# Key chunk 3 of the first stage loaded through ScalarE's queue, and tile 0's keys by four chunks first

## The chip, the cores and the metric

The kernel runs on one core of a Trainium2 chip. The core has TensorE (PE: matmuls, with a separate row PEld for weight loads), VectorE (DVE), ScalarE (ACT), GpSimd (POOL) and SyncE (SP), which here does nothing but issue DMAs. ScalarE issues a few DMAs as well. All DMAs run on the core's 16 DMA engines. The metric is the device time of one execution in microseconds (us); lower is better. Before the change it is 273.6 us, the median of 3 runs (273.55 to 273.61).

## What is computed

x is 2048 x 640, all tensors are bf16. The output mixes two blocks with a gate per row:

```python
g = sigmoid((x * gate_w).sum(-1, keepdims=True))
a = A(x, wqkv, wo)      # linear attention, 32 heads of 20
b = (gelu(x @ w_gate) * (x @ w_up)) @ w_down
out = g * a + (1 - g) * b
```

In A, `x @ wqkv` gives q, k and v. With phi(t) = (t + 1 where t > 0, else exp(t)) + 1e-6, the attention is phi(q) @ (phi(k)^T v), divided by phi(q) @ sum(phi(k)), and then multiplied by wo. Only the keys phi(x @ wk) and the queries phi(x @ wq) of the first few row tiles, and the gate column, matter for this change.

## The kernel before, in words

x is cut into 16 row tiles of 128 rows, and its 640 columns into 5 chunks of 128 (KC). The contraction over the 640 columns is a sum of 5 matmul steps, one for each chunk; chunk k needs the k-th 128 rows of the weight (`load_wk(k)`, 160 KB) and the transposed tile of x. Tile 0 of x is loaded as it is (`load_x(0)`) and transposed by PE (`T`, line 432) and copied back by VectorE; tiles 1 to 15 are transposed by the DMA itself (`load_xT(i)`, line 354).

The work is written out once in program order and sorted into one list for each engine; every operation waits on semaphores for exactly the operations whose results it needs, and each DMA has its own semaphore. So the order of the calls in the source is the order in which each engine works, and each engine takes its list strictly in order: a PE step that waits for a load holds up all PE steps behind it. The loads without `"act"` are issued by SP, those with `"act"` by ScalarE's queue.

The stages: the start (warm-up matmuls, tile 0's transposes, lines 510 to 514), then the keys of tiles 0 to 3 and the queries of tiles 0 to 3 (KM and QM, lines 451 to 479), then keys and queries together for tiles 4 to 15 (KQ, line 538), then the products of keys with x, the small matrices, the gated feed-forward block (line 706) and the output (line 880). Keys and queries of a tile use two banks of PSUM each (`slot`), eight banks for four results in flight; after the last chunk ScalarE takes the exponential (`phi1`, line 481) and VectorE the maximum (`phi2`, line 491).

`KM(n, ks)` is the step to follow: for tile n (n below 4) and each chunk k in `ks` it issues two matmuls, 512 and 128 columns wide (lines 459 and 460), with the transposed tile as the weights. It waits for the tile's transposed load and for the key chunks in `ks`. `gate_col` (line 502) is one small matmul that needs the gate vector and sets a column of the query weights that all query matmuls wait for. Before the change the loads that matter stand in this order:

- SP: x tile 0, key chunk 0, transposed tile 1, key chunk 3, key chunk 4, transposed tiles 2 and 3, the five query chunks, transposed tiles 4 to 15, and then the large weights.
- ScalarE: a small load of 16 rows (line 368), key chunks 1 and 2, one exponential that brings in its table (line 379), the gate vector (line 381).

And PE's order: chunks 0, 1, 2 of tile 0; chunks 0, 1, 2 of tile 1; chunk 3 of tile 0, chunk 3 of tile 1; the gate column; chunk 4 of tile 0, chunk 4 of tile 1; then tiles 2 and 3 whole.

Of the kernel before, what the change touches and what calls it, by code (L numbers as in the profile page):

```python
# [162 lines left out]
def bass_gated_mix__linear_attn_block__geglu_ffn__prompt_kernel(  # L163
# [63 lines left out]
    with (  # L227
# [8 lines left out]
        with contextlib.ExitStack() as stack:  # L236
# [105 lines left out]
            def dma_in(dst, src, writes, reads=(), eng="sp"):  # L342
                P.op(eng, lambda e, dst=dst, src=src: e.dma_start(dst, src),  # L343
                     reads=reads, writes=writes, dma=new_dma_key())
# [6 lines left out]
            def load_wk(k, eng="sp", after=()):  # L351
                dma_in(wk[:, k, :], A_wqkv[k * 128:(k + 1) * 128, 640:1280], [r_wk[k]], reads=after, eng=eng)

            def load_xT(i, after=()):
                P.op("sp", lambda e: e.dma_start_transpose(xT[:, :, i * 128:(i + 1) * 128],  # L355
                                                           A_x[0, i * 128:(i + 1) * 128, :]),
                     reads=list(after), writes=[r_xT[i]], dma=new_dma_key())
# [12 lines left out]
            load_x(0)  # L370
            load_wk(0)
            load_xT(1)
            load_wk(3)
            load_wk(4)
            load_wk(1, "act")
            load_wk(2, "act")

            zero = nc.const_aps.tensor(0.0, (128, 1), F32)
            P.op("act", lambda e: e.activation(eg[:, 0:1], zero, ACT.Exp), writes=[r_eg[0]])
# [41 lines left out]
            def warm(count, n):  # L421
                def fn(e):
                    last = None
                    for w in range(count):
                        last = e.matmul(ps[:, 4, 0:n], one_l, one_r[:, 0:n], start=True, stop=True)
                    return last
                P.op("pe", fn, writes=[bank[4]])
# [4 lines left out]
            def slot(n):  # L432
                return SLOTS[n % 4]
# [17 lines left out]
            def KM(n, ks):  # L451
                i = seq[n][1]
                b0, b1 = slot(n)

                def fn(e):
                    last = None
                    for k in ks:
                        lhs = xT[:, k, i * 128:(i + 1) * 128]
                        e.matmul(ps[:, b0, :], lhs, wk[:, k, 0:512], start=(k == 0), stop=(k == KC - 1))  # L459
                        last = e.matmul(ps[:, b1, 0:128], lhs, wk[:, k, 512:640],  # L460
                                        start=(k == 0), stop=(k == KC - 1))
                    return last
                P.op("pe", fn, reads=[r_xTa[i] if i < NXN and ks == [0] else r_xT[i]] + [r_wk[k] for k in ks],
                     writes=[bank[b0], bank[b1]])
# [37 lines left out]
            def gate_col():  # L502

                P.op("pe", lambda e: e.matmul(ps[:, 7, 0:5], gw_sb, ident[:, 0:5], start=True, stop=True),
                     reads=[r_gw, r_ident], writes=[bank[7]])
                P.op("dve", lambda e: e.tensor_copy(wq[:, :, 640:641], ps[:, 7, 0:5].unsqueeze(2)),
                     reads=[bank[7]], writes=[r_gcol])
# [4 lines left out]
            T(0, [0], 7)  # L512
            T(0, [1, 2, 3, 4], 6)
            warm(2, 128)
            for k in range(3):
                KM(0, [k])
            for k in range(3):
                KM(1, [k])
            KM(0, [3])
            KM(1, [3])  # L520
            gate_col()
            KM(0, [4])
            KM(1, [4])
            ALLK = list(range(KC))
            for n in range(2 * NQ):
# [419 lines left out]
```

## Time and profile before

| | us |
|---|---|
| median of 3 runs | 273.6 (273.55 to 273.61) |
| the profiled execution | 273.49 |
| its span | 272.2 |
| PE busy | 267.0 |
| DVE busy | 140.9 |
| ACT busy | 76.0 |
| first key matmul (tile 0, chunk 0) | 4.45 |
| first matmul of tile 1's keys | 5.90 |
| first matmul of tile 2's keys | 8.10 |
| first query matmul | 10.82 |

The profiled execution is one run under the hardware profiler; its span runs from the first to the last instruction, and the time outside it is 1.29 us. Times inside the span are counted from its start. In a row of the timeline the columns are start, length, engine, line of the kernel, operation, output and input, count, and in brackets how long the engine was idle before and what ended that. `SPq` and `ACTq` are the queues of SP and ScalarE, whose rows are the issue of a DMA and not the transfer; a row "DMA" in the chain is the time from an issue's start to the landing that released the next step. Line 343 is the helper that all plain loads go through, line 355 that of the transposed ones.

### The profile page before, as it was taken

The numbers are of one execution on the slowest core, as the hardware profiler recorded it, in microseconds if no ns is written. First come the engines' busy times: TensorE is split into PE (matmuls) and PEld (weight loads), VectorE is DVE, ScalarE is ACT, GpSimd is POOL, SyncE is SP. The second block draws the span as 40 slices with busy tenths as digits, with TensorE's granted clock in tenths as the row PEclk, the third lists the DMA queues.
The fourth block names the chain that finished last, engine by engine and source line by source line (L and its number), as shares of the span: only waits on it lengthen the run. The fifth ranks groups of instructions, "written<-read, shape, count | busy, mean of one in ns | idle before, by whom it ended". The sixth has DMA issues, their size and how long they took to land.

```text
span 272.2 us, 3462 instructions
## 1 busy us (share of the span) xinstructions
PE 267.0 (98%) x1366; PEld 127.2 (47%) x1392; DVE 140.9 (52%) x248; ACT 76.0 (28%) x132; POOL 30.6 (11%) x30
## 2 busy tenths in 40 slices
PE   7999999999999999999999999999999999999997
PEld 3555555544445454444444444444444444444444
DVE  1678989997234335999999999634110000000200
ACT  2455555210422453332222232224011122121021
POOL 6000000003240002242332421000000000000000
DMA  7976999610200011614121221262031110110221
GB/s 192 203 117 120 356 401 379 117 3 19 58 19 2 23 52 48 198 28 52 24 48 29 46 48 25 60 233 94 2 78 40 39 39 19 41 39 19 58 60 39
DMA packets 42680, 23.61 MB, mean 87 GB/s; under 512 B 32167, under 2 KB 41255, under 8 KB 42535
## 3 DMA queue, kind: packets, MB, share of 16 engines
q1 hardware_dynamic: 42333, 23.05, 32.2%
q10 hardware_dynamic: 330, 0.33, 0.4%
q8 instruction: 11, 0.18, 0.3%
q14 instruction: 6, 0.05, 0.1%
HBM read 13.67 MB, written 2.63 MB: 60 GB/s over the span
## 4 chain that ended last, share of the span: by engine, by line
PE 96%; DMA 1%; SPq 1%; issue 1%; DVE 0%
PE ps L706 41%; PE ps L880 23%; PE ps L545 12%; PE ps L602 6%; PE ps L859 4%; PE ps L684 2%; PE ps L474 2%; PE ps L827 2%; PE ps L605 1%; DMA pool<-in_A_x_dram 1%; PE ps L459 1%; PE ps L840 1%; SPq L343 1%; SPq L355 0%; PE ps L755 0%
## 5 line engine op out<-in xcount | busy, mean ns | idle before, releaser
L706 PE MATMUL ps<-pool 128*128 128x512 bf16 x509 | 112.8, 379 | 0.7 <-issue 0.2
L706 PEld LDWEIGHTS ps<-pool 128*128 128x128 bf16 x520 | 50.6, 98 | 60.3
L880 PE MATMUL ps<-pool 128*128 128x512 bf16 (+2 forms) x300 | 62.2, 366 | 0.5 <-issue 0.2
L712 ACT ACTIVATE pool<-ps 128x512 f32<-128x512 f32 x52 | 31.1, 597 | 72.8 <-PE ps L706 70.1
L714 DVE TENSOR_TENSOR pool<-ps,pool 128x512 bf16<-128x512 f32 x52 | 34.7, 688 | 31.1 <-PE ps L706 29.8
L880 PEld LDWEIGHTS ps<-pool 128*128 128x128 bf16 x306 | 29.2, 98 | 33.4 <-issue 0.4
L863 DVE TENSOR_TENSOR pool<-ps,pool 128x512 bf16<-128x512 f32 x4 | 2.8, 692 | 61.5 <-PE ps L859 59.4
L545 PE MATMUL ps<-pool 128*128 128x512 bf16 (+1 forms) x176 | 32.5, 343 | 0.2
L770 POOL TENSOR_TENSOR pool<-pool 128x640 f32<-128x640 bf16 x16 | 22.5, 1406 | 72.6 <-DVE pool L772 65.8
L887 ACT ACTIVATE pool<-ps,pool 128x512 bf16<-128x512 f32 (+1 forms) x16 | 10.9, 681 | 68.6 <-PE ps L880 68.6
L545 PEld LDWEIGHTS ps<-pool 128*128 128x128 bf16 x180 | 17.6, 98 | 15.0
L564 DVE SCALAR_TENSOR_TENSOR pool<-ps,pool 128x128 bf16<-128x128 f32 (+2 forms) x36 | 21.7, 603 | 2.1
L555 ACT ACTIVATE pool<-ps 128x640 bf16<-128x640 f32 x24 | 16.9, 704 | 15.8 <-DVE pool L564 9.3
L602 PE MATMUL ps<-pool 128*128 128x512 bf16 x76 | 19.2, 379 | 0.1
L780 DVE TENSOR_TENSOR pool<-pool 128x640 bf16<-128x640 bf16 x16 | 13.2, 825 | 0.6
L778 DVE TENSOR_SCALAR pool<-pool 128x32 f32<-128x32 f32 x16 | 12.8, 802 | 0.6
L772 DVE TENSOR_REDUCE pool<-pool 128x32 f32<-128x640 f32 x16 | 12.9, 807 | 0.0
L650 DVE TENSOR_TENSOR pool<-pool 128x640 f32<-128x640 f32 x14 | 11.6, 825 | 0.5
L859 PE MATMUL ps<-pool 128*128 128x512 bf16 x51 | 11.4, 379 | 0.0
L652 POOL PARTITION_ALL_REDUCE pool<-pool x1 | 4.0, 3972 | 60.2 <-DVE pool L650 60.2
L602 PEld LDWEIGHTS ps<-pool 128*128 128x128 bf16 x78 | 6.9, 98 | 7.3
L561 DVE TENSOR_SCALAR pool<-pool 128x640 bf16<-128x640 bf16 x24 | 7.8, 326 | 1.7 <-ACT pool L555 0.4
(73 smaller groups left out, 123.4 us busy)
## 6 DMA issues: line engine op xcount, KB each, us to landing
out_dram<-pool SPq DMA_DIRECT2D x19, 128.0 KB, 1.7
pool<-in_B_w_gate_dram SPq DMA_DIRECT2D x1, 2080.0 KB, 14.3
pool<-in_B_w_up_dram SPq DMA_DIRECT2D x1, 2080.0 KB, 18.4
pool<-in_A_wqkv_dram SPq DMA_DIRECT2D x8, 160.0 KB, 3.0
pool<-in_A_x_dram SPq DMA_DIRECT2D x1, 1280.0 KB, 9.3
pool<-in_A_x_dram SPq DMA_DIRECT2D x1, 1120.0 KB, 6.4
pool<-in_B_w_down_dram SPq DMA_DIRECT2D x1, 1120.0 KB, 6.2
pool<-omg_row SPq DMA_DIRECT2D x1, 1024.0 KB, 4.8
```

The source lines that it names most:

```text
L545: last = e.matmul(ps[:, b + p, 0:c1 - c0], xT[:, k, i * 128:(i + 1) * 128], wkq[:, k, c0:c1], start=(k == 0), stop=(k == KC - 1))
L555: P.op("act", lambda e: e.activation(e_buf[m], ps_flat[:, o:o + 640], ACT.Exp), reads=banks, writes=[r_e[m]])
L564: P.op("dve", lambda e, c0=c0, c1=c1: e.scalar_tensor_tensor(dst[:, c0:c1], ps_flat[:, o + c0:o + c1], 1.0 + EPS, e_buf[m][:, c0:c1], ALU. ...
L602: last = e.matmul(ps[:, b, :], pk[i][:, c * 128:(c + 1) * 128], x_aug[:, i, 0:512], start=(i == 0), stop=(i == NT - 1))
L706: last = e.matmul(ps[:, b, :], w[:, k, fc * 128:(fc + 1) * 128], xT[:, k, j * 512:(j + 1) * 512], start=(k == 0), stop=(k == KC - 1))
L712: P.op("act", lambda e: e.activation(ge[n], ps[:, gb, :], ACT.Gelu_apprx_tanh), reads=[bank[gb]], writes=[r_ge[n]])
L714: P.op("dve", lambda e: e.tensor_tensor(hT[fc][:, j * 512:(j + 1) * 512], ps[:, ub, :], ge[n], ALU.mult), reads=[bank[ub], r_ge[n]], write ...
L770: P.op("pool", lambda e: e.tensor_tensor(tmp[n], pq[i], z_b, ALU.mult), reads=[r_pq[i], r_zb], writes=[r_tmp[n]])
L772: P.op("dve", lambda e: e.tensor_reduce(den[n], tmp[n].rearrange("p (h d) -> p h d", h=32), AX.X, ALU.add), reads=[r_tmp[n]], writes=[r_de ...
L780: P.op("dve", lambda e: e.tensor_tensor(pq[i].rearrange("p (h d) -> p h d", h=32), pq[i].rearrange("p (h d) -> p h d", h=32), den[n].unsqu ...
L859: last = e.matmul(ps[:, b, :], wd[:, fc, 512:640], hT[fc][:, j * 512:(j + 1) * 512], start=False, stop=(fc == NFC - 2), skip_group_check=True)
L880: last = e.matmul(ps[:, pb, 0:c1 - c0], lhs, rhs, start=False, stop=(q == len(rows) - 1), skip_group_check=True)
```

## The change

Two edits. Key chunk 3 is issued by ScalarE's queue, behind chunks 1 and 2 and ahead of the table's exponential and the gate vector; SP issues chunk 4 directly behind the transposed tile 1. PE's order of the first two tiles becomes chunks 0 to 3 of tile 0, chunks 0 to 3 of tile 1, chunk 4 of tile 0, the gate column, chunk 4 of tile 1. The matmuls and the loads are the same ones, and so many.

```diff
@@ -370,10 +370,10 @@
             load_x(0)
             load_wk(0)
             load_xT(1)
-            load_wk(3)
-            load_wk(4)
             load_wk(1, "act")
             load_wk(2, "act")
+            load_wk(3, "act")
+            load_wk(4)
 
@@ -512,14 +512,13 @@
             T(0, [0], 7)
             T(0, [1, 2, 3, 4], 6)
             warm(2, 128)
-            for k in range(3):
+            for k in range(4):
                 KM(0, [k])
             for k in range(3):
                 KM(1, [k])
-            KM(0, [3])
             KM(1, [3])
+            KM(0, [4])
             gate_col()
-            KM(0, [4])
             KM(1, [4])
```

## The prediction

> **What bounds the kernel now.** I read the page first, for what the whole is limited by; then the chain that ended last, in its first 20 us, where the edited lines lie; then the timeline of SP, ACT and PE there; last the DMA view, cut into short windows. The page says:
>
> ```profile
> span 272.2 us, 3462 instructions
> ...
> PE 96%; DMA 1%; SPq 1%; issue 1%; DVE 0%
> ```
>
> TensorE (PE) makes 96% of the chain of work that ended last (and its busy row has 267.0 us, 98% of the span). The change neither adds nor removes a matmul, so only PE's waits can move the time. The chain shows the one that counts:
>
> ```profile
> 3.06 0.57 SPq L343
> 3.64 0.04 issue
> 3.68 0.43 SPq L343
> 4.11 0.04 issue
> 4.15 3.90 DMA pool<-in_A_x_dram
> 8.05 0.05 issue
> 8.10 0.39 PE ps L459
> ```
>
> Columns are start, length, what. SP, done with the transposed load of x tile 1 (issued from 1.71 to 3.01), issues key chunk 3 (3.06), key chunk 4 (3.68) and x tile 2 (4.15). Tile 2 lands 3.90 us after its issue began, at 8.05, and from 8.10 on the chain is PE alone, apart from 0.05 us steps. Whatever the change is worth stands in the place of that 8.10: the first matmul of tile 2's keys. PE's timeline has the waits before it:
>
> ```profile
> 5.26 0.22 PE L460 MATMUL ps<-pool 128*128 128x128 bf16 x1
> 5.90 0.39 PE L459 MATMUL ps<-pool 128*128 128x512 bf16 x1 [0.42 <-DMA pool<-in_A_x_dram]
> ...
> 6.18 0.38 PE L459 MATMUL ps<-pool 128*128 128x512 bf16 x1
> ...
> 7.78 0.22 PE L460 MATMUL ps<-pool 128*128 128x128 bf16 x1
> ...
> 8.09 0.10 PEld L459 LDWEIGHTS ps<-pool 128*128 128x128 bf16 x1 [0.43 <-DMA pool<-in_A_x_dram]
> ```
>
> Tile 0's first three chunks end at about 5.31; tile 1 lands at 5.85 and its first matmul starts at 5.90; one chunk of one tile takes 6.18 - 5.90 = 0.27 us; the last of the first seven chunks and the gate column ends at about 7.84, and PE then idles until tile 2 is there. The third thing to see is what the DMA engines do meanwhile. q1 is SP's queue, q10 ScalarE's; the columns are packets, MB and time as a share of 16 engines, first in the window from 4.00 to 4.25, then from 4.5 to 5.0:
>
> ```profile
> q10 hardware_dynamic: 55, 0.06, 65.5%
> q1 hardware_dynamic: 79, 0.02, 35.5%
> ```
>
> ```profile
> q1 hardware_dynamic: 393, 0.12, 127.3%
> ```
>
> and all queues together, in the last two columns here (DMA share, GB/s):
>
> ```profile
> 3.00:5.00 2.00, 1.52 (x13) 0.98 (x11) 0.65 (x2) 0.68 (x2) 1.67 (x7) 1.00 1.10 303
> 5.00:5.50 0.50, 0.48 (x4) 0.14 (x2) 0.00 (x0) 0.00 (x0) 0.43 (x1) 1.00 0.96 226
> 5.50:6.85 1.35, 0.95 (x7) 0.57 (x8) 0.00 (x0) 0.00 (x0) 0.00 (x0) 1.00 1.02 257
> ```
>
> From 3.0 to 6.85 the engines' share is 0.96 to 1.10: what waits there waits for engines, not for an issue.
>
> **The change part by part.** First, SP's queue. Chunk 3's issue, 0.57 + 0.04 us, goes, but chunk 4 now comes straight behind the transpose and takes over the 0.57 that the first plain load there cost, in place of 0.43. So tile 2's issue starts at 3.68 and not 4.15: 0.47 us earlier, and with it tile 3 (5.39 to 4.92), the five query chunks and the twelve transposes behind them. These later ones are hidden in either case: tile 3's keys start at 9.47, more than a step after tile 2's, and the query matmuls at 10.82, and no PE wait on a load is listed after 8.10. Without that cover the 0.47 would be a gain there, not a cost.
>
> Second, ScalarE's queue. The two plain loads issued there took 0.93 us together from 1.23, so chunk 3 is issued at about 2.17 and holds ScalarE's queue 0.47 us. Behind it are the table load (2.20, becomes 2.67, ends 3.95), the gate vector's DMA (2.27, becomes 2.74) and one exponential of a zero (3.49, becomes 3.96). The next ScalarE work is at 7.76 after 4.07 us of idle, which hides all of it; with no such idle it would cost the 0.47. The gate vector's few packets were read by 5.0 (no packet of q10 after that); 0.47 later and behind 128 more packets they are read by about 6, and the gate column, which PE reaches at about 7.6, has more than 1 us to spare. Were that gone, PE would wait, and with it chunk 4 of tile 1.
>
> Third, the landing of chunk 3. ScalarE's two chunk loads landed 3.3 us after their issue, so chunk 3 lands at about 2.17 + 3.3 = 5.47 instead of behind tile 1. The new order puts tile 0's fourth chunk ahead of tile 1: it starts at about 5.5, ends at 5.78, and lies in the idle stretch from 5.31 to 5.90. That takes 0.27 us out of what PE still has to do after tile 1's landing: 7.84 - 5.90 - 0.27 = 1.67 us. Chunk 4 (SP's loads of this kind took 3.1 us: 3.06 + 3.1 = 6.2) is wanted about 1.1 us after tile 1's first matmul, so it isn't the last to come.
>
> Behind it on the way to PE's query work stand ScalarE's exponential and VectorE's maximum of tile 1 (VectorE ends at 10.77, PE needs the bank at 11.10): 0.33 to spare, of which a later end of tile 1's keys (7.92 in place of 7.84, below) takes 0.08.
>
> So tile 2's first matmul starts at the later of two moments: tile 2's landing + 0.05, or tile 1's landing + 0.05 + 1.67. Before, the first was 8.10. The second breaks even when tile 1 lands at 6.38.
>
> Fourth, tile 1's landing. Its 640 packets of 256 bytes were read on q1 up to about 5.0, the last half us with q10 nearly empty. Now chunk 3's 128 packets stand on q10 beside them. In the mixed slice above q10 moved 55 packets and q1 79 in 0.25 us; alone, q1 moved 393 in 0.5, or 197 in 0.25. 128 packets at 55 per 0.25 us take 0.58 us, in which q1 loses (197 - 79) x 0.58 / 0.25 = 274 packets, 0.35 us at its own rate. Tile 1 then lands at 6.20. The ends: no delay (5.85), if chunk 3 is fitted in; and all 640 packets at the mixed rate, 640 / 79 x 0.25 = 2.03 in place of 1.24 us, 0.79 late (6.64). I take 0.35, since it is the two measured rates. PE's second moment is then 6.20 + 1.72 = 7.92.
>
> Fifth, tile 2's landing. Low end: it keeps its 3.90 us from issue, 3.68 + 3.90 = 7.58 (the shortest landing of any transpose of x, 3.0, would make it 6.68, and tile 1 then decides). High end: the transposes lose 0.79 to the shared queues and get back nothing, 8.05 + 0.79 = 8.84. Between: what the engines must move before tile 2 is the same bytes in both kernels (tile 0, five key chunks, tile 1, only one of them on another queue), and the engines were occupied all through, so it lands where it did; the unused 4% of 5.0 to 5.5 is 0.02 us. I take 7.95, near to that end, since occupied engines are what the rows show, with a tenth of a us off for the slow 226 GB/s of that stretch, which a second queue might fill. Start of tile 2's keys: the later of 8.00 and 7.92, so 8.00, a gain of 0.1 us.
>
> Here a rule stands against the purpose of such a move. The rows are the engines' shares of 0.96 to 1.10 above. The Trainium skill, page "DMA: Bandwidth & Descriptors", section "Issuing engines are not separate DMA queues", says that loads issued from different engines end up on the same 16 DMA engines and that a second issuer saves only issue time. By the page alone the gain is at most the saved issue, 0.47 us, and nothing where the engines are the limit.
>
> The sum: the profiled execution took 273.49 (span 272.2 and 1.29 around it), 0.11 below the median of 273.6. 273.49 - 0.1 = 273.39, or 273.5 in terms of the median.
>
> **The rivals.** First: tile 2 follows its issue after all. For it speaks that transposes landed between 3.0 and 4.4 us after issue (median 3.6), whatever the queue held, so the 3.9 of tile 2 is not the least. Then the start is the later of 7.63 and tile 1's 7.57 to 7.92: gains of 0.2 to 0.47 us, 273.1 to 273.4. To be faster by over 0.2% (0.55 us, about what a measurement of this kernel can tell from no change) tile 1 would have to land before 5.83 too; with both at the median 3.6 (5.3 and 7.28) the start would be 7.33 and the time 272.85. Against: tile 1 gets more company, not less.
>
> Second, on the other side: the transpose pays for the shared engines twice. Chunk 3's packets hold up tile 1 by the upper 0.79, and since tile 2 stands behind tile 1 on q1, it is late by as much while the place chunk 3 left on q1 brings nothing. Tile 2 lands at 8.84, its keys start 0.79 later: 274.4. It loses from a landing of tile 2 past 8.05 on, and shows past 8.60. For it: 0.5 us after tile 1's packets (5.0 to 5.5) only 226 GB/s moved with engines at 0.96, so a transpose leaves something behind that slows others. Against: the place on q1 is a whole chunk of 128 packets.
>
> Third: it doesn't do what it says, chunk 3 landing so late on ScalarE's queue that tile 0's fourth chunk, now ahead of tile 1, holds PE. It costs only past 8.10 - 0.05 - 1.67 - 0.27 = 6.11, 0.64 later than expected; before, chunk 3 came from SP 3.2 us after a later issue. At 6.5 it would be 0.4 slower: 274.0.
>
> PE's clock is no rival with a price: it idled 0.48 us before the first key matmul (4.45) and 0.42 before 5.90 and each chunk after it still took 0.27; the new idle, 5.78 to 6.25, is as long.
>
> **How the numbers follow.** Forecast, start between 7.8 and 8.3 (273.3 to 273.8): 0.5. First rival: 0.2, half past the bound. Second: 0.22, nearly all past the bound. Third: 0.08, half past it at its end. So faster 0.1, same 0.65, slower 0.25. The range reaches to the first rival's lower part and the second's price: 272.95 to 274.4, which leaves some 0.15 outside. The forecast's own range is 273.3 to 273.8.
>
> **What would show it.** Right: chunk 3's issue in ScalarE's queue at 2.2; SP's transpose of tile 2 at 3.7; tile 0's fourth chunk on PE at about 5.5, before the wait for tile 1; tile 1's first matmul near 6.25; tile 2's near 8.0; all later PE work shifted by the same. Wrong: tile 2's first matmul below 7.6 (issue was the limit) or above 8.6 (second rival), a wait of PE on a key chunk after 6.1 (third), or any difference that arises after 20 us, where I expect only a shift.

## The result, and the profile after

The changed kernel takes 274.51 us (median of 14 runs, 273.88 to 278.61) against 273.5 before (14 runs, 273.14 to 273.66). The ratio is 1.0049, with a 95% interval of 1.003 to 1.0067: it is 0.49% slower. The ratio leaves out the run of 278.61, which counts as slow, and it is not the ratio of the two medians, which are 0.37% apart. Two things are to be explained: the median, and the spread, since the 14 runs before lie within about 0.5 us and those after within several. Four of the five runs at 275.5 and above were recorded with a mean granted clock of 0.994 or 0.988, all others with 1.00.

The profiled execution took 274.37 us. Its page has

```profile
span 273.1 us, 3462 instructions
...
PE 96%; DMA 2%; issue 1%; ACTq 0%; DVE 0%
```

so the span is 0.9 us longer and the DMA has 2% of the chain that ended last instead of 1%. That chain, in its first us (start, length, what):

```profile
1.71 0.46 ACTq L343
2.20 4.64 DMA pool<-in_A_wqkv_dram
6.88 0.39 PE ps L459
```

It no longer leads through SP and tile 2 but through ScalarE's queue: key chunk 3 is issued there at 2.20, as planned, and lands 4.64 us later, at 6.84. PE's timeline shows who waits:

```profile
5.29 0.39 PE L459 MATMUL ps<-pool 128*128 128x512 bf16 x1 [0.19 <-DMA pool<-in_A_wqkv_dram]
5.52 0.22 PE L460 MATMUL ps<-pool 128*128 128x128 bf16 x1
6.88 0.39 PE L459 MATMUL ps<-pool 128*128 128x512 bf16 x1 [1.15 <-DMA pool<-in_A_wqkv_dram]
...
8.52 0.17 PE L504 MATMUL ps<-pool 128*128 128x5 bf16 x1
...
8.82 0.38 PE L459 MATMUL ps<-pool 128*128 128x512 bf16 x1
```

The row at 6.88 is tile 0's chunk 3, which PE now has ahead of all of tile 1. The matmul at 8.82 is the first of tile 2's keys, the one that stood at 8.10: 0.72 us later. The first query matmul moved from 10.82 to 11.54, also 0.72, and the shift stays at 0.71 up to 49 us. There, at the start of the products of keys with x, the span gains another 0.15 us (the wait of PE's weight load for VectorE is 0.47 and not 0.15). That step also turns up in the run with tile 1 loaded plainly, below, which loses nothing in the first stage, so I don't count it as a part of the loss.

The landings in this execution, for what was issued around 2.2 us (KB each, us from issue to landing):

```profile
pool<-in_A_wqkv_dram ACTq DMA_DIRECT2D x1, 160.0 KB, 4.6
pool<-in_A_x_dram SPq DMA_TRANSPOSE x1, 5.3
```

Before, ScalarE's chunk loads took 3.3 us and tile 1's transpose 4.1. Both are late now, by 1.3 and 1.2 us. What the two queues did from 4.25 to 5.75 us (packets, MB, time as a share of 16 engines):

```profile
q1 hardware_dynamic: 588, 0.17, 65.2%
q10 hardware_dynamic: 129, 0.15, 62.3%
```

and the window of all queues (last two columns: DMA share, GB/s), first after, then before:

```profile
4.25:5.75 1.50, 1.15 (x6) 0.39 (x6) 0.01 (x1) 0.00 (x0) 1.04 (x3) 1.00 1.28 213
```

```profile
4.25:5.75 1.50, 1.03 (x6) 0.43 (x6) 0.00 (x0) 0.00 (x0) 1.05 (x3) 1.00 1.15 262
```

62.3% of 16 engines over 1.5 us is 14.95 us for 129 packets: 116 ns for one, on average over the queue, whose packets are mostly the 1280-byte rows of the chunks. In the slice that the prediction took its rate from, before the change, it was 65.5% of 16 x 0.25 us for 55 packets, 48 ns. So the queue's packets took 2.4 times as long, and the engines moved less in all, 213 GB/s against 262, while they counted as busier (1.28 against 1.15).

### The profile page after: what moved, and what is told of

Same layout as the page of the kernel before. It is cut to its first block, busy times and chain, and to the rows that moved or that the text cites. A ratio compares the mean times of both kernels' runs of the same rounds, so it can differ in the third digit from the quotient of the medians.

```text
span 273.1 us, 3462 instructions
## 1 busy us (share of the span) xinstructions
PE 267.1 (98%) x1366; PEld 127.1 (47%) x1392; DVE 140.8 (52%) x248; ACT 75.9 (28%) x132; POOL 30.6 (11%) x30
## 4 chain that ended last, share of the span: by engine, by line
PE 96%; DMA 2%; issue 1%; ACTq 0%; DVE 0%
PE ps L705 41%; PE ps L879 23%; PE ps L544 12%; PE ps L601 6%; PE ps L858 4%; DMA pool<-in_A_wqkv_dram 2%; PE ps L683 2%; PE ps L474 2%; PE ps L826 2%; PE ps L604 1%; PE ps L459 1%; PE ps L839 1%; PE ps L754 0%; PE ps L475 0%; PE ps L460 0%
```

## The experiments

Two theories of the lateness stood against each other at first: the loads (the chunk on ScalarE's queue and the transpose on SP's slow each other), and PE's order (chunk 3 of tile 0 put ahead of tile 1). A third cause, PE's clock, came in with the spread.

### The load alone

```diff
 # the kernel before, with
-            load_wk(3)
-            load_wk(4)
             load_wk(1, "act")
             load_wk(2, "act")
+            load_wk(3, "act")
+            load_wk(4)
```

> Only the load is moved; PE keeps the order of before. Theory (the chunk on ScalarE's queue and the transpose of tile 1 on SP's queue slow each other down on the shared engines): both land late again, tile 1 near 7.0 us, so PE waits at tile 1 instead of at chunk 3, from 5.3 to about 7.05, then 1.95 us of work: tile 2's keys start near 9.0 and the time is 0.9 us over before, about 274.4. Rival (PE's new order is to blame, since it puts chunk 3 ahead of tile 1): without the order there is no loss, 273.5, and tile 1 lands by 6.2.

275.16 us (274.36 to 277.68), ratio 1.0073 (1.0045 to 1.0101). Tile 1 landed 5.30 us after its issue, at 7.01:

```profile
7.06 0.61 PE L459 MATMUL ps<-pool 128*128 128x512 bf16 x1 [0.63 <-DMA pool<-in_A_x_dram]
```

The moved load makes both late without the new order. In this execution PE also ran at half its rate until about 8.3 (see the next section), so the 275.16 holds a second loss besides the late landing. Whether the new order is better or worse than the old one with the moved load isn't shown: the intervals of the two ratios overlap.

### PE's order alone

```diff
 # the kernel before, with
-            for k in range(3):
+            for k in range(4):
                 KM(0, [k])
             for k in range(3):
                 KM(1, [k])
-            KM(0, [3])
             KM(1, [3])
+            KM(0, [4])
             gate_col()
-            KM(0, [4])
             KM(1, [4])
```

> Only PE's order is changed; the loads are those of before. Theory (loads): chunk 3 lands at 6.22 as before, PE starts it at 6.27 and then has 1.95 us of work, so tile 2's keys start at 8.22 instead of 8.10: 0.12 us slower, 273.6. Rival (order): most of the 1.0 us loss, 274.4.

273.81 us against 273.56 in the same series; ratio 1.0028 (1.0007 to 1.0049). Seven of the twelve runs lie at 273.64 to 273.82, which is the small loss expected, and five at 275.18 to 275.75, with nothing between. The profiled execution was one of the upper five, and shows what that one is:

```profile
4.80 0.63 PE L459 MATMUL ps<-pool 128*128 128x512 bf16 x1
...
5.33 0.63 PE L459 MATMUL ps<-pool 128*128 128x512 bf16 x1
...
6.46 0.61 PE L459 MATMUL ps<-pool 128*128 128x512 bf16 x1 [0.38 <-DMA pool<-in_A_wqkv_dram]
6.86 0.31 PE L460 MATMUL ps<-pool 128*128 128x128 bf16 x1
6.96 0.63 PE L459 MATMUL ps<-pool 128*128 128x512 bf16 x1
7.39 0.31 PE L460 MATMUL ps<-pool 128*128 128x128 bf16 x1
7.50 0.63 PE L459 MATMUL ps<-pool 128*128 128x512 bf16 x1
```

One chunk of one tile takes 7.50 - 6.96 = 0.54 us where it took 0.27: PE still runs at half its rate here, and does so until about 10 us. It did so before the new order made any difference, too: 5.33 - 4.80 = 0.53 for a chunk of tile 0. (The granted clock, PEclk, reads 1.00 throughout in this execution's records, so "half its clock" is read from the spacing of the matmuls.) From 6.46 on, six chunks at 0.53 in place of 0.27 cost 1.6 us; the upper group lies 1.4 to 2.1 us above the lower. So the order isn't the cause of the late landing (chunk 3 landed at 6.41 here), but it brings out a second effect.

The kernel before has runs at that height as well: over all its series 11 of 135 lie above 275, against 5 of 12 here. No profile shows what those 11 are.

### The clock: PE kept busy in its wait

```diff
 # the kernel with PE's order alone changed, with
-            for k in range(4):
+            for k in range(3):
                 KM(0, [k])
+            warm(2, 512)
+            KM(0, [3])
```

> The kernel with only PE's order changed (runs at 273.64 to 273.82 and others at 275.2 to 275.75), with two warm-up matmuls of 512 columns ahead of tile 0's chunk 3, where PE waits for it. If the upper group is PE's full clock coming later because PE idles longer here, the upper group vanishes and all runs lie at 273.6 to 273.9. If it has another cause, some 5 of 12 runs stay above 275.

273.84 us, all twelve runs at 273.6 to 274.37; ratio 1.0000 (0.9985 to 1.0015). The upper group is gone. Two matmuls that compute nothing of use, put where PE would have waited, take away the loss by the ratio; its interval still overlaps that of the kernel without them. The median is 0.2 us above the 273.61 of that series, about the small loss expected. The same in the changed kernel, with five of them:

```diff
 # the changed kernel, with
-            for k in range(4):
+            for k in range(3):
                 KM(0, [k])
+            warm(5, 512)
+            KM(0, [3])
```

> The changed kernel with five warm-up matmuls of 512 columns (5 x 0.216 = 1.08 us) ahead of tile 0's chunk 3, in the stretch in which PE waited from 5.55 to 6.88. If the idle PE lets its clock drop in some executions (those at 275 to 276.5 us), these vanish and the runs lie together at 274.0 to 274.5, with a median at or a little below the changed kernel's 274.5. If the clock has no part in it, the spread stays.

274.57 us (274.1 to 275.24); ratio 1.0026 (1.0009 to 1.0043) in place of 1.0049. The runs at 275.5 and above are gone, but the lower ones are no faster, and chunk 3 was later still (its first matmul at 7.78 in the profiled execution). By the two ratios, 0.23% of the 0.49%, or 0.6 us, would go with the idle PE, and 0.26%, or 0.7 us, with the late landing itself. The second is near the shift of 0.72 in the profile, but the intervals of the two ratios overlap, so this split is an estimate.

The granted clock points the same way. Over all kernels here 14 runs were recorded with a mean below 1.00, all of kernels in which PE's new or longer wait was left empty. None of the 57 runs of the five kernels with a filled wait is among them, and none of the 121 of the kernel before in the series of the experiments.

The changed kernel once more shows both at once:

> The changed kernel once more, for a second look at its landings. Chunk 3 and tile 1 were there at 6.83 and 7.02; in the run with warm-ups they came at 7.73 and 7.93. If the clash is of varying length, they come somewhere between 6.5 and 8.0 and the start of tile 2's keys follows chunk 3 by 2.0 us; if the warm-ups delayed them, they come at 6.8 and 7.0 again.

275.79 us. Chunk 3 and tile 1 landed at 7.04 and 7.25, and PE was at half its rate until about 9.6:

```profile
7.08 0.61 PE L459 MATMUL ps<-pool 128*128 128x512 bf16 x1 [0.61 <-DMA pool<-in_A_wqkv_dram]
7.48 0.31 PE L460 MATMUL ps<-pool 128*128 128x128 bf16 x1
7.59 0.63 PE L459 MATMUL ps<-pool 128*128 128x512 bf16 x1
...
10.24 0.38 PE L459 MATMUL ps<-pool 128*128 128x512 bf16 x1
```

The last row is tile 2's first key matmul, 2.14 us later than before the change. I had expected it 2.0 us behind chunk 3, which holds only at the full clock; here it is 3.2.

### Is it the transpose?

```diff
 # the changed kernel, with
-            load_xT(1)
+            dma_in(xT[:, :, 128:256], A_x[0, 128:256, :].rearrange("p (k s) -> p k s", k=KC), [r_xT[1]])
```

> The changed kernel, but tile 1 of x comes by a plain DMA of the same 640 pieces of 256 bytes, untransposed, so tile 1's keys and queries are computed from untransposed data. Theory (it is the transpose that clashes with the other queue): chunk 3 lands at about 5.5 and tile 1 by 6.2, tile 2's keys start near 8.0, 273.4. Rival (any 640 small packets beside the chunk do it): chunk 3 at 6.8 as in the changed kernel, 274.5.

The same number of pieces of the same size on the same queue, only not transposed. The issue on SP takes 0.67 us and not 1.31, so chunk 4 and tile 2's transpose are issued about 0.6 us earlier too; that brings chunk 3 more company, not less. 274.12 us, above the 273.4 expected; ratio 1.0025 (1.0004 to 1.0046). Three of the ten runs are the upper ones, at 274.93 to 276.13. Chunk 3 landed at 6.03, as the chain shows,

```profile
2.19 3.84 DMA pool<-in_A_wqkv_dram
```

and in the window from 4.25 to 5.75 the queues and the sum were

```profile
q1 hardware_dynamic: 784, 0.30, 76.4%
q10 hardware_dynamic: 178, 0.18, 35.3%
```

```profile
4.25:5.75 1.50, 1.11 (x6) 0.39 (x6) 0.06 (x1) 0.00 (x0) 1.04 (x3) 1.00 1.12 325
```

35.3% x 24 us / 178 is 48 ns for a packet, and 325 GB/s moved in place of 213. Tile 2's keys started at 8.02. So about 0.5 us of chunk 3's lateness (6.03 against the 5.5 expected) is plain sharing of the engines, and the other 0.8 to 1.0 needs the transpose. With two warm-up matmuls in the wait:

```diff
 # the last one, with
-            for k in range(4):
+            for k in range(3):
                 KM(0, [k])
+            warm(2, 512)
+            KM(0, [3])
```

> As the run with tile 1 loaded plainly (tile 1's keys and queries computed from untransposed data), with two warm-up matmuls of 512 columns ahead of tile 0's chunk 3, so that PE's clock plays no part. Theory (the transpose makes the chunk late): chunk 3's packets take about 56 ns again, it lands at 6.0, and the runs lie at 273.4 to 273.9 in one group, 0.7 or more below the changed kernel with its wait filled (274.57). Rival (the one look was chance): packets of 120 ns, chunk 3 past 6.8, 274.2 to 275.

273.9 us, eleven of twelve runs at 273.52 to 274.25 and one at 275.86; ratio 1.0009 (0.9991 to 1.0026). The packets took 48 ns again, 333 GB/s moved, chunk 3 landed at 6.1. Compared with 274.57 for the changed kernel with its wait filled, in another series, the transpose beside the chunk is worth about 0.7 us.

### Whose transpose

Tile 2's transpose is issued 0.47 us earlier in the changed kernel, so two transposes come close behind each other on SP's queue. Two kernels ask whether that matters: one more plain load between chunk 4 and tile 2, and tiles 2 and 3 loaded untransposed.

```diff
 # the changed kernel, with
             load_wk(4)
+            dma_in(wv[:, 0, :], A_wqkv[384:512, 640:1280], [r_wv])
```

> The changed kernel with one more plain load of 160 KB on SP's queue behind chunk 4 (into the place of the value weights), so that tile 2's transpose is issued at 4.15 as before the change and not at 3.68. Theory A (chunk 3 clashes with tile 1's own transpose): nothing gained, chunk 3's packets take 120 ns and more and it lands at 6.8 or later; 274.4 to 275. Theory B (the clash comes from the second transpose being issued and queued so soon behind the first): chunk 3's packets take about 55 ns, it lands by 6.1 and tile 1 by 6.3; the time is then set by tile 2, some 0.4 later than before for the additional bytes: 273.9 to 274.1.

275.97 us (four runs, 274.43 to 276.73), ratio 1.0097 (1.0078 to 1.0116); chunk 3 at 6.89, its packets at 72.7% x 24 / 127 = 137 ns.

```diff
 # the changed kernel, with
             for i in range(2, NQ):
-                load_xT(i)
+                dma_in(xT[:, :, i * 128:(i + 1) * 128],
+                       A_x[0, i * 128:(i + 1) * 128, :].rearrange("p (k s) -> p k s", k=KC), [r_xT[i]])
```

> The changed kernel, but tiles 2 and 3 of x come by plain DMAs of the same pieces, untransposed, so their keys and queries are computed from untransposed data; tile 1 is transposed as in the changed kernel. Theory A (tile 1's own transpose): chunk 3's packets take 120 ns and more, it lands at 6.8 or later, tile 2's keys start at 8.8 or later: 274.3. Theory B (the second transpose behind it): about 55 ns, chunk 3 by 6.1, tile 1 by 6.3, tile 2's keys at 8.0: 273.4 to 273.6.

274.87 us (six runs, 274.5 to 276.33), ratio 1.0056 (1.0034 to 1.0078); chunk 3 at 7.27, its packets at 112 ns. Both speak for tile 1's own transpose. This last execution also shows the clock in the records themselves (windows; PE busy first after the length, PEclk third from the end):

```profile
3.62:7.03 3.41, 1.44 (x11) 0.51 (x8) 0.48 (x2) 0.54 (x2) 1.53 (x5) 1.00 1.12 224
7.03:10.44 3.41, 3.12 (x12) 1.48 (x13) 0.00 (x0) 0.00 (x0) 0.00 (x0) 0.50 1.16 303
10.44:13.85 3.41, 3.41 (x28) 1.96 (x27) 2.55 (x6) 2.16 (x4) 0.00 (x0) 1.00 1.06 204
```

PE was busy for 1.44 of 3.41 us, and for the next 3.41 us the granted clock was a half; then it was full again. One such stretch makes a mean of 0.994 over the span, which is what the record has for this run and for three of the upper runs of the changed kernel. So the second effect has two forms: the full rate comes late, where the records read 1.00 all the same, or it is withdrawn for a while. The Trainium skill, page "TensorE: Matmul & The Clock Gate", section "Part 1: The HAM clock gate (the "warmup" mystery)", speaks of a free-running activity window of 3413 ns and of an idle window after which the clock is halved. The length agrees with the stretch at half clock here. But in the stretch of the same length just before it PE was busy for 42% of the time, so if that was the window, it need not be idle all through, and the measurement decides.

### An additional load on the second queue

```diff
 # the kernel before, with
             load_wk(2, "act")
+            dma_in(wv[:, 0, :], A_wqkv[384:512, 640:1280], [r_wv], eng="act")
```

> The kernel before, with one more load of 160 KB on ScalarE's queue behind chunks 1 and 2 (the bytes of chunk 3 into the place of the value weights, overwritten later); SP's queue and PE's order are as before. Theory (a third plain load on the second queue beside the transpose slows the transpose): tile 1 lands at about 7.0 instead of 5.85, PE waits there until 7.05, tile 2's keys start at 9.0 or later: 274.4 to 274.8. Rival (plain cost of 160 KB more bytes on the engines): 0.4 us later at most, 274.0 or less, and tile 1 by 6.25.

275.84 us (274.29 to 277.99), ratio 1.0082 (1.0052 to 1.0112). The time is above even the theory's 274.4 to 274.8, but the profiled execution (275.39) doesn't show the clash: tile 1 landed at 6.49, and the packets of the queue took 41.4% x 24 / 194 = 51 ns. The added load's packets were read from about 4.9 on, when most of tile 1 had been read, so the two hardly overlapped. PE ran at half its rate there until about 9.2, so most of this execution's loss is the second effect: tile 1 landed 0.64 us later than before the change, and tile 2's keys started 1.70 later, at 9.80. With four warm-up matmuls ahead of tile 1's keys:

```diff
 # the last one, with
+            warm(4, 512)
             for k in range(3):
                 KM(1, [k])
```

> As the run of the kernel before with one more load behind chunks 1 and 2 on ScalarE's queue, with four warm-up matmuls of 512 columns ahead of tile 1's keys. Theory (a third plain load beside the transpose makes the transpose late whoever needs the load): its packets take 120 ns or more in most executions, tile 1 lands at 7.0, 274.3 to 274.8 in one group. Rival (only the additional bytes count): packets near 60 ns, tile 1 at 6.5 or before, tile 2's keys at 8.5, 273.9 to 274.1.

275.03 us (274.18 to 276.76), ratio 1.0046 (1.0016 to 1.0077). Here the packets took 128 ns, and tile 1 came 5.96 us after its issue:

```profile
7.72 0.39 PE L460 MATMUL ps<-pool 128*128 128x512 bf16 x1 [0.82 <-DMA pool<-in_A_x_dram]
```

So the clash varies from one execution to the next, and a third plain load of this size can bring it about even when PE needs nothing of it. That all runs would lie in one group was missed: three of nine are above 276. PE still idled for 0.82 us after the warm-ups, which may be why; it isn't shown.

### Two chunks on each queue

```diff
 # the changed kernel, with
             load_wk(0)
+            load_wk(1)
             load_xT(1)
-            load_wk(1, "act")
             load_wk(2, "act")
             load_wk(3, "act")
```

> The changed kernel, but key chunk 1 goes back to SP, ahead of tile 1's transpose; ScalarE's queue carries chunks 2 and 3 only, so two chunks as before. Theory (the clash is the third chunk, still being read when the transpose runs): the packets of ScalarE's queue end near 4.5, chunk 3 lands by 5.0 as chunk 2 did, tile 1 is issued 0.46 later and lands near 6.3, tile 2's keys start at 8.1: 273.5 to 273.7. Rival (chunk 3 on ScalarE's queue is late by itself): 274.4 as in the changed kernel.

274.41 us (273.51 to 275.4), ratio 1.0027 (1.0007 to 1.0046): six runs at 273.51 to 273.97, as before the change, and six at 274.85 to 275.4. Chunk 3's packets took 22.5% x 24 / 119 = 45 ns, and it landed at 5.85, 0.85 later than I had expected but in time; tile 2's keys started at 8.17. With three warm-up matmuls behind tile 0's chunk 0, where PE waits for chunk 1:

```diff
 # the last one, with
-            for k in range(4):
+            KM(0, [0])
+            warm(3, 512)
+            for k in range(1, 4):
                 KM(0, [k])
```

> As the run with chunk 1 back on SP ahead of tile 1's transpose and chunks 2 and 3 on ScalarE's queue (lower group 273.51 to 273.97, upper 274.85 to 275.4), with three warm-up matmuls of 512 columns behind tile 0's chunk 0, where PE waits for chunk 1. If the upper group is the clock alone, all runs lie at 273.5 to 274.0. If not, half of them stay above 274.8.

273.83 us, ten of twelve runs at 273.46 to 274.13 and two at 275.3 and 276.4; ratio 1.0012 (0.9991 to 1.0033). The profiled execution was the slowest of them: PE waited 1.29 us for chunk 0, ahead of the warm-ups, and ran at half its rate until about 10. So chunk 3 may go through ScalarE's queue without a measurable loss when that queue carries two chunks and not three and the wait is filled. It isn't faster than the kernel before, though.

### Tile 1 transposed by PE

If the DMA's transpose is what hurts, tile 1 can be loaded plainly and transposed by PE, as tile 0 is.

```diff
 # the changed kernel, with
-NXN = 1
+NXN = 2
...
-            load_xT(1)
+            load_x(1)
...
-            for k in range(4):
+            for k in range(3):
                 KM(0, [k])
+            T(1, [0], 7)
+            T(1, [1, 2, 3, 4], 6)
+            KM(0, [3])
```

> The changed kernel's loads, but tile 1 of x is loaded plainly by SP and transposed by PE as tile 0 is (five small PE transposes and two copies by VectorE, ahead of tile 0's chunk 3); the DMA's first transpose is then tile 2's. Theory (the chunk on ScalarE's queue is late only because of the transpose beside it): its packets take about 48 ns instead of 116 to 128, chunk 3 lands by 5.6, tile 1 by 5.0, PE idles little, and tile 2's keys start at 7.3 to 7.7: 272.8 to 273.2, faster than before, and without runs above 275. Rival (ScalarE's queue is slow with a third chunk whatever lies beside it): chunk 3 at 6.8, 274.4.

274.98 us (274.0 to 276.07), ratio 1.0041 (1.002 to 1.0063). The packets did take 51.4% x 24 / 256 = 48 ns, and 371 GB/s moved, the most of all; but chunk 2 landed only at 5.89 and chunk 3 at 6.6:

```profile
5.94 0.61 PE L459 MATMUL ps<-pool 128*128 128x512 bf16 x1 [0.37 <-DMA pool<-in_A_wqkv_dram]
```

SP now has two more plain loads in front (tile 1 and chunk 4), and ScalarE's chunks share the engines with them from the start. I had counted on the absence of the clash and forgotten the sharing. This execution (276.02) also ran at half its rate until about 10; the lower runs, 274.0 to 274.4, are no faster than before either. With chunk 3 back on SP:

```diff
 # the last one, with
-            load_wk(3, "act")
+            load_wk(3)
```

> As the last one, but chunk 3 stays on SP's queue, ahead of chunk 4, as before the change. It shows what the move of chunk 3 is worth when no transpose of tile 1 is there. Theory: SP's issue of tile 2 is 0.47 later than with chunk 3 on ScalarE's queue, so tile 2's keys start up to 0.47 us later: 273.0 to 273.5. Rival (issue is hidden by the engines even then): the same time as the last one within 0.1 us.

274.37 us (273.71 to 276.03), ratio 1.0022 (1.0003 to 1.0042). Chunk 2 landed at 6.04 and set PE's pace again, so tile 2's issue had no chance to count. Both are slower than the kernel before; no version tried here beats it.

### What stays open

The packets on ScalarE's queue in the window from 4.25 to 5.75, worked out as above (one profiled execution for each; the averages count a few small packets of the queue too):

| kernel | ns for a packet | that load lands at | GB/s |
|---|---|---|---|
| changed, and once more | 116, 128 | 6.8, 7.0 | 213, 210 |
| changed, wait filled | 147 | 7.7 | 142 |
| load alone | 112 | 7.0 | 216 |
| one more load before tile 2 | 137 | 6.9 | 202 |
| tiles 2, 3 untransposed | 112 | 7.3 | 208 |
| additional load, without and with warm-ups | 51, 128 | 6.4, 7.4 | 298, 182 |
| tile 1 untransposed, without and with warm-ups | 48, 48 | 6.0, 6.1 | 325, 333 |
| two and two, without and with warm-ups | 45, 45 | 5.9, 6.3 | 283, 217 |

The transposed load and a third chunk beside it belong to every slow row; the additional load's first execution had both and was not slow. Why the engines slow down is not shown. In the kernel before and in the two-and-two versions the other queue's packets overlapped the transpose too, and were not slow; there they came early in it. The plain packets that followed the transpose on its own queue before the change were slow as well, 226 GB/s between 5.0 and 5.5; whether that is the same thing, and when exactly the slow phase begins, wasn't tried.

## Why the prediction was wrong

The forecast was 273.5 us, within 0.2% of before; measured are 274.51, 0.1 above the upper end of the range, 274.4.

- **What bounds the kernel:** right. No matmul was added, PE's waits before tile 2's keys decided, and the first-stage shift went through to the end of the span.
- **SP's queue and ScalarE's queue:** right. Tile 2's transpose was issued at 3.68, chunk 3 at 2.20, and the table load and the gate vector (2.68 and 2.76) were covered.
- **Chunk 3's landing, "2.17 + 3.3 = 5.47":** this is the step that failed. It landed at 6.84. The 3.3 us was the landing of two loads of which all but 26 packets had been read by 4.25, early in the transpose; the third was read beside the rest of it. Of the 1.4 us that were missing, the plain-tile run gives about 0.5 to the sharing, and the other 0.8 to the transpose.
- **Tile 1's landing, 6.20:** failed in the same way, 7.01, beyond even the upper end of 6.64. The step took the mixed rate, 55 and 79 packets in 0.25 us, from the first half us of the transpose. Later in it the chunk's packets take 116 ns and not 48, and the transpose's own rate falls with them (q1 read 263 packets from 4.5 to 5.0, and 393 before the change).
- **Tile 2's landing, 7.95:** right by the number, 3.68 + 4.3 = 7.98, but no longer what decides. The reason given, the same bytes on engines as busy as before, did not hold from 4.25 to 5.75, where 213 GB/s moved and not 262; so a part of this is luck.
- **The formula for the start of tile 2's keys:** right. The third rival said that chunk 3 costs what it lands past 6.11: 6.84 - 6.11 = 0.73, measured 0.72. I gave it 0.08 and had the chunk at 6.5 at worst. The second rival named the right disturbance, a transpose that leaves something behind, but charged it to tile 2, which was not late.
- **"PE's clock is no rival with a price":** failed. The new idle stretch was 1.2 us and not 0.5, and with such a stretch left empty the full clock came late or was withdrawn in some executions: by the estimate above 0.6 us of the 1.3 that the ratio stands for, and most of the spread (274.1 to 275.24 with the wait filled).

The rows before the change already held a sign of this that the prediction didn't read:

```profile
0.82 2.40 PE L425 MATMUL ps<-const-bfloat16-1.0 128*128 128x512 bf16 x6 [0.82 <-PEq L930]
...
4.45 0.43 PE L459 MATMUL ps<-pool 128*128 128x512 bf16 x1 [0.48 <-DMA pool<-in_A_wqkv_dram]
...
4.77 0.38 PE L459 MATMUL ps<-pool 128*128 128x512 bf16 x1
```

The six warm-up matmuls (five of 512 columns and one of 128) took 2.40 us, some 0.43 for 512 columns where a later one takes 0.22, and the first key chunk took 4.77 - 4.45 = 0.32 and not 0.27. So the full rate had only just come when the keys began.

## What to carry to other kernels

A landing time read from a trace belongs to the company that the load had: before moving a load to a second queue, look at what will be on the first one's engines while it is read, and above all whether that is a transpose. A step put first in an in-order engine's list has to have its latest landing priced, not its usual one. And where PE idles early in a kernel, price not only the wait but the clock, over several runs: two matmuls of no use in the wait took the ratio of the order-only kernel from 1.0028 to 1.0000.

## What the runs showed of the hardware that I had not expected

A plain load and a DMA transpose on two queues can slow each other far beyond their bytes: the packets of the plain load's queue, mostly of 1280 bytes, at 112 to 147 ns in place of 45 to 51, and 142 to 216 GB/s in all in place of 325 and more with the same pieces untransposed. And PE's full clock at the start of a kernel is not certain: by the spacing of the matmuls it came at about 4 us in some executions and as late as about 10 in others, and once it was given and withdrawn again for 3.41 us after a stretch in which PE was busy for 1.44 us of 3.41.
